# Every written order of a two-part kernel replaced by another: emission, engine sequences and the slots of rotating tiles

## The chip, the core and the metric

The kernel runs on one core of a Trainium2 chip. The metric is the time of one execution on the device in microseconds (us); the lower the better. Five engines take part: TensorE (PE, with its weight loads as PEld), VectorE (DVE), ScalarE (ACT), GpSimd (POOL) and SyncE (SP), which here only issues transfers. Each engine takes its instructions strictly in its own written order and waits, where data or a buffer is not there, with everything behind the waiting instruction.

## What is computed

Two independent results are put side by side. Part A is attention over a short window with 32 heads: each position looks at eight earlier positions, two apart. Part B is a convolution along the sequence whose kernel is a sum of 192 decaying complex exponentials per channel.

```python
def _A_ref(x, wqkv, wo):                    # x: 1 x 2048 x 640, 32 heads of 20
    q, k, v = ...                           # x @ wqkv
    idx = pos[:, None] - (jnp.arange(8) * 2)[None, :]
    logits = jnp.einsum("bhsd,bhswd->bhsw", q, kg) * scale
    attn = _softmax(jnp.where(mask, logits, -1e9), axis=-1)
    o = jnp.einsum("bhsw,bhswd->bhsd", attn, vg)
    return o @ wo

def _B_ref(u, A_re, A_im, B_re, B_im, C_re, C_im, log_dt, Dskip):
    logdA, dB = dt * A, dt * Bc             # 640 channels x 192
    P = jnp.exp(logdA[:, :, None] * l)      # l = 0 .. 2047
    K = jnp.einsum("dn,dnl,dn->dl", Cc, P, dB).real
    y = irfft(rfft(u padded) * rfft(K padded))[:L]
    return y + u * Dskip

return jnp.concatenate([a, b], axis=-1)
```

## The kernel before, in words

The program is cut into small pieces of work, each for one engine, and each belongs to a stage. A stage's name carries its block or chunk number: `logits2` is the attention logits of the third block of 512 positions, `kgen43` the fourth quarter of the convolution kernel of the fifth chunk of 128 channels.

Stages of part A: `x0..3` load the input transposed; `k`, `q`, `v` with a number project 512 positions (five groups of five matmuls and evictions each, line 747) and store them to device memory; `fetch` reads the q and k rows of a block back in five tiles through three rotating buffers (`qk`, line 767), `fetchv` the v rows (line 780); `logits` makes ten products on VectorE (line 793), which TensorE sums (line 800), then a maximum, an exponential and a division (lines 808 to 828); `av` makes ten products of v and the attention weights on VectorE (line 842), summed by TensorE (line 850); `out` is the output projection (line 867). The products of `logits` and `av` go through three rotating buffers (`pr`).

Stages of part B: `prep`, `weights`, `am0/am1`, `gens0/gens1`, `genm0/genm1` make the exponentials at powers of two: a phase and its absolute value on VectorE (lines 477 and 479), two sines on ScalarE (lines 478 and 480) and a product with the magnitude on VectorE (line 488). Set 0 is for the first chunk and stays on the chip, set 1 for the other four goes through device memory (`Gdram`). The temporary tiles of these stages rotate through four buffers (`tmp4`). For each chunk c of five, `tab` and `taby` read the generators back, `xtab` and `ypos` multiply them up to two tables (Xtab has two buffers, Ytab only one), `mag` and `yneg` add Ytab's other half (lines 557, 562 and 563). `kgen` (lines 596 and 603) contracts the tables on TensorE in four quarters of two pieces each; a piece is 64 small matmuls, the first with four more. `kd` shifts the result between partitions by four transfers (line 584); `spread` (lines 637, 642 and 658) and `spec` (lines 678 and 683) take it to the frequency domain, as `u` does with the input; `swap` exchanges halves by a transfer (line 1073); `prod` (lines 688 and 689) multiplies the spectra, `inv` (line 703) and the `last` stages (lines 1131 and 1134) go back, with constants that `hb` loads (HB, eight transfers of 512 KB, line 1103) and an input product `ud` (line 1112).

What sets the order is written out by hand in three constants. `TRACE` is the order in which pieces are emitted; it sets the program's data dependencies and which buffer a rotating tile follows. `SEQ` is each engine's order (`.P` TensorE, `.A` ScalarE, `.V` VectorE, `.G` GpSimd, `.S` SyncE; `:4` means four pieces in a row). `SLOTS` says, for each use of a rotating tile in the order of emission, which buffer it takes.

```python
    def slot(self, pool, tag, bufs, shape, dt, name):
        k = self.used.get(tag, 0)
        self.used[tag] = k + 1
        i = int(SLOTS[tag][k]) if tag in SLOTS else k % bufs
        return pool.tile(shape, dt, name=name, tag=f"{tag}{i}", bufs=1)
    ...
    def chain(self, text):
        ...
                for ins in next(left[stage, engine]):
                    if engine in last:
                        self.tc.add_manual_dep(ins, last[engine].name, ...)
                    last[engine] = ins
    ...
    op.trace(TRACE, dict(attpool=attention_pool, fftpool=fft_pool, invpool=inv_pool))
    op.chain(SEQ)
```

Three words in `TRACE` (`attpool`, `fftpool`, `invpool`) are places where a memory pool gives way to another.

Of the kernel before, what the change touches and what calls it, by code (L numbers as in the profile page):

```python
# [127 lines left out]
def att_consts_np():  # L128
# [13 lines left out]
ypos0.G params.A params.S params2.G params.A params.S params2.G params.A params.S params2.G params.A params.S params2.G params.A params.S  # L142
params2.G:2 params.S prep.A params.A params2.G prep.V x0.S params2.G:2 params.S params2.G prep.V:2 x0.S prep.V params2.G prep.V prep.P prep.V
params2.G prep.P prep.A x0.S params2.G weights.P mag0.A params2.G mag0.A:2 params2.G mag0.A x0.S prep.P mag0.A params2.G mag0.A prep.P mag0.A prep.V
mag0.A ypos0.G weights.P mag0.A wk.S load.G mag0.A prep.V load.G mag0.A x0.S weights.P prep.V mag0.A load.G mag0.A weights.P mag0.A prep.V mag0.A
load.G weights.P mag0.A x1.S weights.A prep.V load.G weights.P weights.A gens0.V load.G prep.V weights.P weights.A gens0.V x1.S load.G prep.V
weights.V weights.A weights.P am0.A load.G prep.V am0.A weights.V am0.A wq.S load.G am0.A:2 x1.S set.G weights.V am0.A set.G am0.A:2 weights.V
am0.A:2 load.G x1.S weights.V am0.A prep.A weights.V load.G k0.P weights.S gens1.V load.G x2.S gens1.V load.G gens0.A gens1.A load.G gens1.V gens0.A
k0.P load.G gens1.A gens1.V load.G x3.S gens1.A weights.V gens1.A gens1.V k0.P genm0.V k0.A gens1.V x1.S gens1.A q0.P weights.V k0.A wv.S gens1.A
gens1.V q0.P weights.V x2.S q0.A gens1.V q0.P gens1.A x2.S weights.V k0.A q0.P weights.V gens1.A gens0.V x2.S weights.V q0.A q0.P gens0.V gens0.A  # L150
gens0.V gens0.A gens0.V q0.A weights.S k0.P gens0.V genm0.V gens0.A x2.S gens0.V gens0.A gens0.V gens0.A k0.P genm0.V gens0.A gens0.V gens0.A
gens0.V gens0.A x3.S genm0.V k0.A gens0.V:2 k0.A genm0.V gens0.V gens0.A xtab0.V k0.S v0.P gens0.A v0.P gens0.A gens0.V x3.S xtab0.V gens0.A xtab0.V
q0.A gens0.V:2 v0.P q0.A genm0.V gens0.V gens0.A xtab0.V q0.S gens0.A:2 gens0.V k1.P x3.S xtab0.V gens0.A gens0.V gens0.A gens0.V gens0.A xtab0.V
gens0.V gens0.A k1.P genm0.V gens0.A x3.S genm0.V xtab0.V k1.P xtab0.V genm0.V v0.A xtab0.V k1.P v0.A xtab0.V genm0.V v0.A xtab0.V k1.P v0.P genm0.V
xtab0.V am1.A xtab0.V v0.P v0.A genm1.V am1.A xtab0.V genm1.S v0.A k1.A v0.S q1.P:2 k1.A genm1.V k1.A q1.P k1.A gens1.V k1.A xtab0.V q1.P am1.A k1.S
xtab0.V genm1.S am1.A xtab0.V q1.P am1.A genm1.V v1.P am1.A xtab0.V genm1.S q1.A v1.P q1.A gens1.V q1.A v1.P xtab0.V q1.A genm1.V q1.A v1.P am1.A
q1.S xtab0.V genm1.S am1.A gens1.V k2.P xtab0.V am1.A k2.P xtab0.V am1.A v1.A gens1.V k2.P am1.A xtab0.V v1.A k2.P xtab0.V v1.A ypos0.V v1.A k2.P
ypos0.V k2.A ypos0.V:2 k2.A v1.P k2.A:2 ypos0.V k2.A ypos0.V v1.A k2.S q2.P yneg0.V q2.P v1.S q2.P gens1.A ypos0.V gens1.A q2.P gens1.A gens1.V q2.P
genm1.V q2.A:2 gens1.V v2.P genm1.S q2.A:2 ypos0.V q2.A v2.P gens1.A q2.S v2.P gens1.A gens1.V genm1.V gens1.A v2.P gens1.V v2.A genm1.S v2.A v2.P
genm1.V gens1.A k3.P gens1.V v2.A genm1.S ypos0.V v2.A:2 k3.P gens1.V gens1.A v2.S q3.P gens1.V gens1.A genm1.V gens1.A q3.P gens1.V genm1.S gens1.A  # L160
q3.P genm1.V gens1.A k3.A gens1.V genm1.S q3.P q3.A genm1.V q3.A q3.P gens1.V q3.A genm1.S q3.A ypos0.V k3.P q3.A gens1.A q3.S yneg0.V v3.P gens1.A
v3.P k3.A genm1.V k3.A v3.P yneg0.V genm1.S attpool fetch0.S v3.P gens1.A mag1.A fetch0.S v3.A:2 v3.P v3.A mag1.A:2 kgen03.P tab1.S mag1.A:2 wo.S
mag1.A:2 fetch0.S mag1.A k3.P mag1.A logits0.V fetchv0.S mag1.A:2 fetchv0.S mag1.A k3.P mag1.A fetchv0.S logits0.V mag1.A:3 k3.A kgen03.P logits0.V
fetch0.S k3.A v3.A k3.S logits0.P v3.A kgen02.P xtab1.V kgen03.A v3.S fftpool logits0.V fetchv0.S xtab1.V:2 logits0.V xtab1.V:5 logits0.P xtab1.V
kgen00.P xtab1.V:2 kgen00.P logits0.V xtab1.V:2 logits0.V u0.S fetch0.S xtab1.V u0.S logits0.P kgen00.A kgen01.P xtab1.V:2 u0.S xtab1.V kgen01.P
xtab1.V logits0.V u0.S xtab1.V:2 logits0.V logits0.P fetch1.S kgen01.A kgen02.P xtab1.V:2 kgen02.A ypos1.G taby1.S logits0.V ypos1.G taby1.S:2
xtab1.V logits0.P taby1.S xtab1.V taby1.S logits1.V T.S u0.P logits0.A u0.P kd0.S u0.A u0.P ypos1.V kd0.S u0.P u0.A logits1.V fetch1.S u0.P u0.A
u0.P fetchv0.S u0.P u0.A kd0.S ypos1.V u0.P ypos1.V u0.A logits0.V kd0.S u0.A u1.S ypos1.V u0.A:2 logits0.V ypos1.V logits0.P ypos1.V logits0.V
ypos1.V logits0.P spec.P logits0.A spec.P:2 spec.A fetchv0.S spec.A ypos1.V spec.P spec.A:2 spec.P spec.A tab2.S spec.A spec.P spec.A wo.S spec.A
logits1.V spread0.P fetch1.S spread0.P spec.A spread0.P spread0.A spread0.P fetch1.S spread0.A ypos1.V u1.S spread0.A ypos1.V spec.A:3 logits0.P  # L170
yneg1.V spread0.A spec.P:2 spec.A spread0.P spec.A spread0.P:2 spread0.A spread0.P yneg1.V spread0.P spec.A spread0.P spec.A spread0.P logits0.A
spread0.P mag2.A logits0.P mag2.A xtab2.V mag2.A u1.S logits0.A yneg1.V logits0.A mag2.A xtab2.V mag2.A kgen13.P xtab2.V mag2.A logits0.V mag2.A:3
wo.S mag2.A kgen13.P xtab2.V mag2.A swap0.S mag2.A:2 xtab2.V fetchv0.S xtab2.V mag2.A xtab2.V mag2.A u1.S spread0.A xtab2.V spread0.A xtab2.V
# [132 lines left out]
010101001011  # L306
# [883 lines left out]
```

## Time and profile before

| | |
|---|---|
| median of three runs | 370.8 us (368.31, 371.45, 370.8) |
| span of the profiled execution, first to last instruction | 368.0 us |
| that execution's own time outside the span | not given; the lowest of the three runs is 0.3 us above the span |
| TensorE busy, mean granted clock | 292.8 us, 0.903 |
| VectorE busy | 305.1 us |
| ScalarE busy | 257.2 us |
| transfers | 65.5 MB, mean 178 GB/s |

In the rows shown below, a line of the timeline has the start and the duration in us, the engine, the source line, the operation with its output and inputs, how many instructions are merged, and in brackets the idle time of the engine ahead of it with what ended that wait. "issue" there is a wait for nothing that the profile shows. SPq is the queue of transfers that SyncE issues; L12 is line 12 of the kernel.

### The profile page before, as it was taken

What the parts mean: (1) busy time and instruction counts of PE and PEld (TensorE: products, weight loads), DVE (VectorE), ACT (ScalarE), POOL (GpSimd) and SP (SyncE); (2) the same over time, 40 slices, a digit from 0 to 9 for tenths busy, and PEclk for the clock granted to TensorE, in tenths of its full rate; (3) what the DMA queues carried; (4) which work ended last, traced back from release to release, by engine and by line L of the source; (5) the groups of instructions that cost most, each with busy time, mean ns of one, the idle gap of its engine ahead of it and who ended that gap; (6) DMA issues with size and microseconds to landing.
All of it is one profiled execution on the core that took longest, in us unless ns stands there. A gap on an engine that the chain in (4) does not pass through costs nothing. (4 is left out here: it accounts for less than half of the span.)

```text
span 368.0 us, 13345 instructions
## 1 busy us (share of the span) xinstructions
PE 292.8 (80%) x5808; PEld 195.3 (53%) x5808; DVE 305.1 (83%) x397; ACT 257.2 (70%) x574; POOL 35.6 (10%) x72
## 2 busy tenths in 40 slices
PE   2959999999654486777989796888988748889984
PEld 1414444445431375555666564567855546557763
DVE  1896999795899988998999998799999935568940
ACT  2978899898600588357999645797779304779773
POOL 9740000000000000000000000000000000002750
PEclk9978999999665678899999899997999966999999
DMA  7999683697978987566976355860768756999885
GB/s 152 204 205 213 185 269 117 202 287 228 263 140 147 238 210 134 139 161 95 205 99 156 121 133 109 228 150 15 142 213 235 257 209 101 190 219 192 227 191 136
DMA packets 119210, 65.49 MB, mean 178 GB/s; under 512 B 76192, under 2 KB 115712, under 8 KB 118000
## 3 DMA queue, kind: packets, MB, share of 16 engines
q1 hardware_dynamic: 116320, 61.61, 71.6%
q0 software_dynamic: 1776, 2.79, 3.7%
q8 instruction: 45, 0.74, 0.9%
q10 hardware_dynamic: 1056, 0.25, 0.3%
q14 instruction: 13, 0.11, 0.1%
HBM read 35.25 MB, written 21.03 MB: 153 GB/s over the span
## 5 line engine op out<-in xcount | busy, mean ns | idle before, releaser
L747 PE MATMUL ps_p<-xT,w 128*128 128x512 bf16 x300 | 69.9, 397 | 4.1 <-DMA w<-in_A_wqkv_dram 4.1
L603 PE MATMUL ps_k<-Ytab,Xtab 64*20 64x33 bf16 (+1 forms) x2560 | 52.9, 247 | 11.7 <-issue 11.7
L842 DVE TENSOR_TENSOR p<-vb,attn 128x2048 bf16<-128x2048 bf16 x40 | 47.5, 1218 | 12.4 <-PE ps_o L850 10.3
L603 PEld LDWEIGHTS <-Xtab 64*20 64x20 bf16 (+1 forms) x2560 | 47.6, 123 | 17.0 <-issue 14.7
L793 DVE TENSOR_TENSOR prod<-qk 128x2048 bf16<-128x2048 bf16 x40 | 48.1, 1224 | 10.0 <-DMA qk<-qkd 7.5
L747 PEld LDWEIGHTS <-w 128*128 128x128 bf16 x300 | 30.2, 102 | 43.0 <-issue 6.2
L683 ACT CAST Sp<-ps_f 128x512 bf16<-128x512 f32 (+1 forms) x96 | 43.1, 613 | 7.0 <-PE ps_f L678 6.7
L662 ACT CAST A<-ps_f 128x512 bf16<-128x512 f32 x80 | 41.4, 619 | 7.1 <-PE ps_f L658 6.8
L617 ACT CAST Kd<-ps_k 128x264 bf16<-128x264 f32 x20 | 7.9, 394 | 47.0 <-PE ps_k L603 47.0
L750 ACT CAST st<-ps_p 128x512 bf16<-128x512 f32 x60 | 31.7, 609 | 7.1 <-DMA qkd<-st 3.1
L800 PE MATMUL ps_l<-prod,cGs 128*32 128x512 bf16 x160 | 21.5, 464 | 17.2 <-DVE prod L793 17.1
L678 PE MATMUL ps_f<-A,cT 64*128 64x128 bf16 (+1 forms) x768 | 27.7, 214 | 7.3 <-ACT Sp L683 3.5
L678 PEld LDWEIGHTS <-cT 64*128 64x128 bf16 x768 | 21.6, 98 | 16.4 <-issue 11.3
L706 ACT CAST Z<-ps_ia 128x512 bf16<-128x512 f32 x40 | 21.7, 632 | 5.6 <-PE ps_ia L703 5.6
L850 PE MATMUL ps_o<-p,cHs 64*32 64x256 bf16 x640 | 21.7, 288 | 4.1 <-DVE p L842 4.1
L867 PE MATMUL ps_op<-wo,oT 128*128 128x320 bf16 x160 | 24.4, 300 | 0.3 <-ACT oT L856 0.2
L547 POOL MEMSET Ytab<- 128x192 bf16 x5 | 1.3, 258 | 238.3 <-PE ps_k L603 134.4
L557 ACT ACTIVATE mag<-ta 128x192 bf16<-128x192 f32 x80 | 22.8, 404 | 0.0
L1139 POOL DMA_DIRECT2D out_dram<-ys x24 | 14.4, 608 | 76.8 <-ACT rc L826 70.2
L703 PE MATMUL ps_ia<-cE,Sp 128*128 128x128 bf16 x160 | 20.5, 224 | 0.7 <-DVE Sp L689 0.4
L510 DVE TENSOR_TENSOR krtmp<-Xtab,Xg 128x3072 bf16<-128x3072 bf16 (+1 forms) x15 | 20.3, 1356 | 0.1
L703 PE MATMUL ps_ia<-cE,UT 128*128 128x128 bf16 x160 | 20.4, 224 | 0.0
(113 smaller groups left out, 531.3 us busy)
## 6 DMA issues: line engine op xcount, KB each, us to landing
qk<-qkd SPq DMA_DIRECT2D x20, 263.0 KB
qkd<-st SPq DMA_DIRECT2D x8, 640.0 KB
UT<-Sp SPq DMA_DIRECT2D x10, 512.0 KB
Gdram<-cs SPq DMA_DIRECT2D x11, 384.0 KB
HB<-k_HB SPq DMA_DIRECT2D x8, 512.0 KB
vb<-vd SPq DMA_DIRECT2D x16, 196.5 KB
Xg<-Gdram SPq DMA_DIRECT2D x4, 768.0 KB
Zdram<-Z SPq DMA_DIRECT2D x3, 1024.0 KB
```

The costliest lines, as they stand in the source:

```text
L557: self.op("A", lambda b=b: self.nc.scalar.activation(out=self.mg[b // 8]()[:, b % 8], in_=ta()[:, s], func=ACT.Exp, scale=-16.0 * (b + 1)))
L603: MM(ps()[32 * g:32 * g + 20, i, :], lhsT=X()[k, :, p % 2, col], rhs=Y()[k, :, p % 2, col], start=False, stop=(p == order[3]), tile_positi ...
L662: op("A", lambda q=q, ps=ps: nc.scalar.copy(out=A1()[:].rearrange("p k r s t -> p (k r) s t")[:, :, sig, 8 * q:8 * q + 8], in_=ps()[:]))
L678: nc.tensor.matmul(ps[h]()[:, kk], lhsT=C["T"]()[hs, k, 64 * (1 - r):64 * (1 - r) + 128], rhs=A1()[hs, k, r, s0:s1, :].rearrange("p s t -> ...
L683: op("A", lambda q=q, h=h, ps=ps: nc.scalar.copy(out=Sp()[:, slots, h, :, 4 * q:4 * q + 4], in_=ps[h]()[:].rearrange("p k (s t) -> p s t k ...
L703: nc.tensor.matmul(ps()[:, i], lhsT=X()[:, h, 4 * t:4 * t + 4, :].rearrange("p g k -> p (g k)"), rhs=C["E"]()[:, n_, :], start=(i == 0 and ...
L706: op("A", lambda h=h, tq=tq, ps=ps: nc.scalar.copy(out=Z()[:, :, 16 * h + 4 * tq:16 * h + 4 * tq + 4], in_=ps()[:].rearrange("p t x -> p x ...
L747: nc.tensor.matmul(ps()[:], lhsT=self.w[which]()[:, kt, 128 * ct:128 * ct + 128], rhs=self.xT()[:, kt, 512 * sc:512 * sc + 512], start=(kt ...
L750: op("A", lambda ct=ct, ps=ps: nc.scalar.copy(out=st()[:, ct], in_=ps()[:]))
L793: op("V", lambda ct=ct, wg=wg, pr=pr: V.tensor_tensor(out=pr[wg]()[:], in0=self.qk[b][ct]()[:, 0, HALO:].unsqueeze(1).to_broadcast([128, 4 ...
L842: op("V", lambda t=t, qp=qp, v4=v4: V.tensor_tensor(out=v4(), in0=windows(self.v[b][t]()[:, 2 * qp:2 * qp + 2, 0:PH], 2, 4), in1=at()[:].u ...
L867: nc.tensor.matmul(ps()[:], lhsT=self.oT[b]()[:, t, 128 * s:128 * s + 128], rhs=self.wo_sb()[:, t, 320 * eh:320 * eh + 320], start=(t == 0 ...
```

## The change

All of `TRACE` and `SEQ` is replaced, and the slot strings of `pr`, `ps`, `st` and `tmp4`. The pieces and their number are the same (432 for TensorE, 576 for ScalarE, 397 for VectorE, 68 for GpSimd, 269 for SyncE). `TRACE` is one line longer, so that later source lines are one higher. The diff is long; here are the parts of `SEQ` and `SLOTS` that the prediction speaks of.

```diff
 # TensorE, chunks 2 to 4
-...spread1.P:3 u2.P:6 out0.P u2.P:2 inv0.P:8 spec1.P out0.P:2 ... spec1.P:4 out0.P:2 kgen21.P:2
+spec1.P:2 logits1.P out0.P spec1.P logits2.P spec1.P:4 logits2.P spec1.P kgen22.P:2 kgen23.P:2 kgen20.P:2 kgen21.P:2 u3.P:6 inv1.P u3.P logits2.P u3.P
-...u4.P:5 kgen32.P:2 kgen30.P logits2.P kgen33.P:2 kgen30.P
-logits2.P:2 inv2.P logits2.P inv2.P:7 kgen31.P:2 u4.P:3 av1.P:2 ...
+...spec2.P:5 kgen30.P kgen31.P:2 u4.P kgen30.P kgen33.P:2
+u4.P:5 av1.P:2 inv2.P:4 u4.P av1.P kgen32.P:2 av1.P logits2.P:4 spread3.P:4 ...
-...spec3.P:8 av2.P:3 kgen43.P
-av2.P kgen42.P av2.P kgen40.P:2 kgen42.P kgen41.P:2 kgen43.P av2.P:3 inv3.P av2.P inv3.P logits3.P inv3.P:5 spread4.P:2 ...
+spec3.P av2.P kgen43.P kgen40.P:2 kgen41.P:2 kgen43.P kgen42.P av2.P:2 kgen42.P spec3.P av2.P spec3.P:2 av2.P spec3.P av2.P:3 inv3.P:3 av2.P inv3.P
+out2.P:2 logits3.P out2.P spread4.P:4 out2.P logits3.P out2.P spread4.P:6 logits3.P spread4.P:2 out2.P:3 inv3.P:4 spec4.P logits3.P spec4.P:3
 # ScalarE, start
-params.A:5 prep.A params.A prep.A mag0.A:16 weights.A:4 am0.A:11 prep.A gens0.A ...
+params.A:6 prep.A:2 am0.A:11 mag0.A:5 weights.A mag0.A:11 gens0.A:3 prep.A gens0.A:2 ...
 # VectorE: start, first logits, end
-prep.V:11 gens0.V prep.V gens0.V prep.V weights.V prep.V weights.V:5 ...
+prep.V:10 gens0.V:4 prep.V gens0.V prep.V gens0.V prep.V gens0.V prep.V ...
-... gens1.V ypos0.V yneg0.V genm1.V yneg0.V logits0.V:3
+... genm1.V:2 ypos0.V yneg0.V ypos0.V:2 yneg0.V logits0.V:3 yneg0.V logits0.V
-... yneg4.V:3 av2.V:5 prod3.V:4 av2.V logits3.V:10 ud1.V ud0.V logits3.V:3 prod4.V:4 ud2.V logits3.V ud3.V av3.V:10
+... av2.V yneg4.V av2.V yneg4.V av2.V:2 logits3.V av2.V:5 prod3.V:3 av2.V prod3.V logits3.V:5 ud1.V ud0.V logits3.V:4 ud2.V ud3.V logits3.V:3 prod4.V:4 logits3.V av3.V:10
 # SyncE, HB and the shift of chunk 4
-fetchv3.S:4 hb.S:8 ud.S:2 kd4.S:2 ud.S kd4.S:2 fetch3.S ud.S:2 fetch3.S ...
+fetchv3.S:3 hb.S:4 ud.S kd4.S:2 hb.S:2 ud.S:2 kd4.S:2 hb.S:2 ud.S:3 fetch3.S out2.S ...
 # SLOTS
     "pr":
-01201020102010212012012102102010201021012020120201201201201201201020102012012012
+01201020102010201201201020120120102010201102102102102102121212102010201021021021
     "tmp4":
-012301010120312012031203120312031203120312031203120312
+012301230231023102320323120213012301230123012301230123
```

A "half" of `kgen` in the prediction is one piece: half of a quarter's work.

More of the change, by code (lines that the diff above doesn't have):

```diff
@@ L141 @@
 TRACE = """
[L142 to L149, printed above, removed]
@@ L154 @@
[L154 to L161, printed above, removed]
@@ L268 @@
-xtab4.V:2 logits2.V xtab4.V logits2.V xtab4.V:2 prod2.V xtab4.V:2 prod2.V av1.V logits2.V xtab4.V:2 av1.V xtab4.V prod2.V xtab4.V:2 prod2.V xtab4.V
-logits2.V xtab4.V:4 av2.V xtab4.V:2 av2.V:2 xtab4.V:4 ypos4.V:8 av2.V ypos4.V:2 yneg4.V:3 av2.V:5 prod3.V:4 av2.V logits3.V:10 ud1.V ud0.V
-logits3.V:3 prod4.V:4 ud2.V logits3.V ud3.V av3.V:10 ypos0.G params2.G:16 ypos0.G load.G:9 set.G:2 load.G:7 ypos1.G:2 ypos2.G:2 ypos3.G:2 ypos4.G:2
-last01.G:4 last03.G:3 last11.G:4 last03.G last05.G:4 last13.G:4 last07.G:4 params.S:6 x0.S params.S x0.S:3 wk.S x0.S x1.S:2 wq.S x1.S:2 weights.S
```

260 lines of the change are left out of this document (139 added, 121 removed).

## The prediction, made before the changed kernel ran

> **What bounds the kernel now.** I read the page first, then VectorE's instructions in order of time with the idle time ahead of each, then the same for TensorE, ScalarE and the SyncE queue around every hole, and last the chain that ended last.
>
> ```profile
> span 368.0 us, 13345 instructions
> ...
> PE 292.8 (80%) x5808; PEld 195.3 (53%) x5808; DVE 305.1 (83%) x397; ACT 257.2 (70%) x574; POOL 35.6 (10%) x72
> ...
> DVE 19%; PE 14%; DMA 7%; issue 5%; SPq 3%; ACT 1%; ACTq 0%; DVEq 0%
> ```
>
> VectorE is the fullest engine and leads the chain. As no operation changes, its 305.1 us of work stay, and only its 62.9 us of idle time (368.0 - 305.1) can move. So the prediction is a ledger of VectorE's holes plus what follows its last instruction.
>
> ```profile
> 5.79 0.28 DVE L427 CAST dtf<-dtb 128x5 f32<-128x5 bf16 x1 [5.79 <-ACT dtb L426]
> ...
> 351.88 2.36 DVE L842 TENSOR_TENSOR p<-vb,attn 128x2048 bf16<-128x2048 bf16 x2 [0.33 <-PE ps_o L850]
> 364.38 0.33 ACTq L1185
> ```
>
> VectorE starts at 5.8 and ends at 354.2 (351.88 + 2.36). The last 13.8 us are TensorE's remaining products, ScalarE's last evictions and the stores. Between them lie some 43 us of holes; the parts below take the large ones. The same ledger would be wrong where TensorE or ScalarE is the later one, so each hole is judged by the engine it waits for.
>
> **The change part by part.** Every sequence differs, so I compare the places where VectorE waits. "Cover" is the VectorE work that the written order puts between the instruction that starts a round trip through other engines and the one that needs its result; the hole is round trip minus cover.
>
> *Opening, to the first attention product.*
>
> ```profile
> 13.25 0.60 DVE L435 TENSOR_SCALAR wk<-ps_tr 128x448 f32<-128x448 f32 x1
> ...
> 29.17 0.26 DVE L477 TENSOR_SCALAR ph<-wi 128x192 int32<-128x192 int32 x1 [0.75 <-ACT cs L478]
> ...
> 36.52 0.26 DVE L477 TENSOR_SCALAR ph<-wi 128x192 int32<-128x192 int32 x1 [1.37 <-ACT Xg L478]
> ...
> 86.34 0.96 DVE L488 TENSOR_TENSOR cs<-cs,am 128x1536 bf16<-128x1536 bf16 x1 [0.52 <-ACT cs L480]
> ...
> 92.30 3.57 DVE L793 TENSOR_TENSOR prod<-qk 128x2048 bf16<-128x2048 bf16 x3 [4.13 <-DMA qk<-qkd]
> 96.69 0.56 DVE L510 TENSOR_TENSOR krtmp<-Xg 128x768 bf16<-128x768 bf16 x1 [0.81 <-DMA Xg<-Gdram]
> ```
>
> ```profile
> 88.50 0.95 SPq L767 DMA_DIRECT2D qk<-qkd  x2
> ```
>
> The last genm1 product ends at 87.3; SyncE stores it, then issues the qk fetch at 88.5, and the first product starts at 92.3. The round trip is 5.0 us, and the old order covers it with one instruction (yneg0's third), so 4.13 stay open, and 0.81 more for Xg, fetched behind it. The new order puts five instructions there (the last three of ypos0 and two of yneg0, some 6.3 us), and the fetch still stands right behind genm1's last store. I book -4.9.
>
> Against it: the new order takes gens0 first, and its second range reduction (wk) takes a tmp4 buffer that the first gens0 phase must give back, which needs a sine on ScalarE.
>
> ```profile
> 8.80 4.15 ACT L557 ACTIVATE mag<-ta 128x192 bf16<-128x192 f32 x16
> ...
> 14.65 2.90 ACT L465 ACTIVATE am<-ta 128x192 bf16<-128x192 f32 x11
> ...
> 17.98 1.28 ACT L478 ACT_TABLE_LOAD   x1
> ```
>
> In the new order am0, mag0 and one cast (0.6) stand ahead of the sines: 8.8 + 2.9 + 4.15 + 0.6 + 1.3 = 17.7, so the first sine ends near 18.1. VectorE gets there at 14.5 (13.25 plus two phases and two absolute values), because the weights products that filled this time before now come later. That is a new hole of 3.6, and 1.0 more while ScalarE paces the sines; the old holes at 29.17 and 36.52 (2.1) go. Net +2.5. The opening: -4.9 + 2.5 = -2.4 (bounds -4.9 with all of it covered, +1.5 if ScalarE's pace costs 5 instead of 1).
>
> *Middle, to the end of yneg4.*
>
> ```profile
> 129.61 1.23 DVE L793 TENSOR_TENSOR prod<-qk 128x2048 bf16<-128x2048 bf16 x1 [0.93 <-DMA qk<-qkd]
> ...
> 138.99 1.23 DVE L828 TENSOR_TENSOR attn<-attn,rc 128x1024 bf16<-128x1024 bf16 x1 [1.61 <-ACT rc L827]
> ...
> 171.58 0.56 DVE L510 TENSOR_TENSOR krtmp<-Ytab 128x768 bf16<-128x768 bf16 x1 [1.68 <-DMA Ytab<-Gdram]
> ...
> 225.48 0.56 DVE L510 TENSOR_TENSOR krtmp<-Ytab 128x768 bf16<-128x768 bf16 x1 [0.89 <-DMA Ytab<-Gdram]
> ...
> 231.97 1.23 DVE L842 TENSOR_TENSOR p<-vb,attn 128x2048 bf16<-128x2048 bf16 x1 [2.06 <-PE ps_l L800]
> ```
>
> These are 7.2 us. The loop behind two of them is yneg(c) -> kgen(c) on TensorE -> taby(c+1) into the single Ytab -> ypos(c+1). The prices:
>
> ```profile
> 247.68 2.48 PE L603 MATMUL ps_k<-Ytab,Xtab 128*20 128x33 bf16 x128
> ```
>
> ```profile
> 270.40 0.43 SPq L543
> ...
> 270.88 3.90 DMA Ytab<-Gdram
> ```
>
> A kgen half is 1.3 us where TensorE runs free (2.48 for the products of two, with its opening matmuls); the reload is 0.4 + 3.9. For chunk 2 the new order runs all eight halves together: 8 x 1.3 + 4.3 = 14.7 against 21.6 of cover, so the wait at ypos3 goes; at ypos2 the last half stands ahead of 11.5 of cover, so that wait goes too. For chunk 3 the loop holds six halves (I take 10, between 7.8 free and 12.0 at the slowest pace shown below), six u4, three av1 and four inv2 products (some 6.1) and two more halves (2.6): with the reload 23.0 against 21.9 of cover, a hole of 1.1, which I raise to 2.0 for the start. For chunk 0 it is about even (0.5). The softmax wait of 1.61 stays (cover 11.2, before 10.7), the waits at 129.61 and 231.97 go, and I allow 0.8 for a new one of their kind: 2.0 + 0.5 + 1.6 + 0.8 = 4.9, so -2.3 (bounds -5.6 and +4).
>
> *kgen4.* The dearest hole.
>
> ```profile
> 286.19 0.97 DVE L563 TENSOR_SCALAR Ytab<-Ytab 128x3072 bf16<-128x3072 bf16 x1
> 287.08 5.76 DVE L842 TENSOR_TENSOR p<-vb,attn 128x2048 bf16<-128x2048 bf16 x5
> ...
> 296.41 1.23 DVE L689 TENSOR_TENSOR Sp<-Sp 128x2048 bf16<-128x2048 bf16 x1
> 307.57 1.23 DVE L842 TENSOR_TENSOR p<-vb,attn 128x2048 bf16<-128x2048 bf16 x1 [9.93 <-PE ps_o L850]
> ```
>
> ```profile
> 286.19 5.31 SPq L1103 DMA_DIRECT2D HB<-k_HB  x8
> ```
>
> ```profile
> 199.98 2.32 PE L603 MATMUL ps_k<-Ytab,Xtab 64*20 64x33 bf16 x119
> ...
> 207.40 0.44 PE L603 MATMUL ps_k<-Ytab,Xtab 64*20 64x33 bf16 x13 [1.95 <-issue]
> ...
> 296.19 2.14 PE L603 MATMUL ps_k<-Ytab,Xtab 64*20 64x33 bf16 x116 [3.71 <-issue]
> ...
> 301.84 2.51 PE L603 MATMUL ps_k<-Ytab,Xtab 64*20 64x33 bf16 x128 [3.19 <-issue]
> ```
>
> VectorE had nine instructions to do (five av2, four prod3) and then waited 9.93 for a product buffer, held until TensorE had worked through kgen4. TensorE itself stood 3.71 and 3.19 with no wait that the profile shows, while 4 MB of HB came in. Without HB four halves in a row still took 7.9 us (199.98 to 207.84), 2.0 each: back to back, kgen does not hold 1.3. The new order has seven halves in a row and only three VectorE instructions (3.45 at the pitch of 287.08) to lay over them; four of the eight HB loads come, some 4 us later than before. I take 11.5 for the seven (9.1 free, 14.0 at 2.0). One av2 product and the start add 0.9, so 11.5 + 0.9 - 3.45 = 8.9; behind it spec3's last four now stand between the av2 products that free the buffers, 2.6 more. 11.5 against 9.93: +1.6 (bounds -1 and +6).
>
> *End.*
>
> ```profile
> 316.95 3.68 DVE L793 TENSOR_TENSOR prod<-qk 128x2048 bf16<-128x2048 bf16 x3 [2.47 <-PE ps_l L800]
> 322.73 2.36 DVE L793 TENSOR_TENSOR prod<-qk 128x2048 bf16<-128x2048 bf16 x2 [2.10 <-DMA qk<-qkd]
> ...
> 332.57 0.42 DVE L813 SCALAR_TENSOR_TENSOR m<-m,ps_m 128x256 bf16<-128x256 bf16 x1 [3.75 <-PE ps_m L812]
> ...
> 338.21 1.48 DVE L1112 TENSOR_TENSOR uD<-uD,Dsb 128x2560 bf16<-128x2560 bf16 x1
> ```
>
> Two uD products (2.8 at pitch) leave the stretch between prod4 and av3 for these holes: -2.8. But prod4 waits for spec4, and between the last spread4 product and spec4's first the new TensorE order puts three out2 and four inv3 groups (some 4.3) where one logits3 and one out2 group stood (1.4); the old order has four more out2 groups among spec4's own, so of these 2.9 I book +1.8. Together -1.0 (bounds -4 and +4), and +0.5 for the end behind av3, where TensorE, not VectorE, is the later one.
>
> **The sum:** -2.4 - 2.3 + 1.6 - 1.0 + 0.5 = -3.6, so 364.4 against the span of 368.0. The three runs shown have a median of 370.8, 2.8 above that span (the lowest, 368.3, is 0.3 above); what is around the span does not change, so 370.8 - 3.6 = 367.2.
>
> [...]
>
> ```profile
> q8 instruction: 45, 0.74, 0.9%
> ```
>
> 45 code pages of 16 KB came in. [...]
>
> **The rivals.**
> 1. *kgen at 1.3 everywhere*, the stalls being accidents of that one execution. Then the seven halves take 9.1 (-2.4) and the holes at ypos4 and ypos1 close (-2.5): 367.2 - 4.9 = 362.3. For it: the free pair at 247.68. Against: the stall at 207.40 had no HB beside it.
> 2. *Slower: chunk 4 is starved.* HB's loads delay TensorE's code and chunk 4's shifted rows. The eight halves of before took 19.2 us without the av2 products between them (286.2 to 306.6), 2.4 each; seven at 2.4 are 16.8, +5.3. The second half of the Kd shift now stands on SyncE behind six HB and three uD loads; two HB and two uD (1.66 MB, 9.3 us at the page's mean of 178 GB/s) come right ahead of it, and TensorE has only some 11.4 us of other work before spread4, against 14: +2.6. The six halves of kgen3 at 2.0 add 2.0, kgen0 0.2. 367.2 + 10.1 = 377.3. It decides from some 4 us of issue stalls inside kgen4. For it: both stalls of 3 us and more lie under HB. Against: HB now starts later and in parts.
> 3. *The holes form anew*: the written order is obeyed, but the waits it closes in the middle and the opening come back elsewhere, as each engine takes its order as written however late a transfer is. Without -2.4 and -2.3: 371.9.
>
> **How the numbers follow.** My forecast 0.42 (its own range 363 to 371), rival 1 0.16, rival 2 0.30, rival 3 0.12. A measurement of this kernel can tell about 1% (3.7 us) from no change. The forecast lies on that bound: 0.22 faster, 0.18 within, 0.02 slower. Rival 1 is faster, rival 2 slower, rival 3 0.02, 0.07 and 0.03. Together 0.40 faster, 0.25 same, 0.35 slower. The range runs from 357 (rival 1 with opening and end at their lower bounds: 362.3 - 2.5 - 3.0) to 379 (rival 2 and a third of the end's upper bound).
>
> **What would show it.** Opening: the first product (now line 794) starts near 90 with no wait for qk, and a hole of about 3.6 at 14 to 18. Middle: no wait for Ytab at ypos2 and ypos3, one of about 2 at ypos4. kgen4: seven halves in 11 to 12 us and a hole of 9 behind three VectorE instructions. If these seven take over 15, rival 2 holds; if 9, rival 1. The forecast is wrong in kind if VectorE's holes sum to what they were but lie in places not named here, or if TensorE's end stands far behind VectorE's.

## The result, and the profile after

The changed kernel is slower: 380.01 us median of four runs (379.26 to 382.78) against 370.58 us for before (with a fourth run, 370.36, beside the three listed above), a ratio of 1.0291 with a 95% interval of 1.0226 to 1.0355. Measured again on another chip it stood at 1.0215 (1.0165 to 1.0265). The forecast was 367.2 us, with a range up to 379.0: wrong in sign, and outside the range by 1 us. The ratios here leave out executions that took over 1.5% longer than the fastest of the same kernel (8 of the 12 of early_again, further down), so some differ from the quotient of the medians.

The page of after, span, busy time, chain and two groups of instructions:

```profile
span 377.5 us, 13318 instructions
...
PE 297.8 (79%) x5808; PEld 198.9 (53%) x5808; DVE 304.4 (81%) x397; ACT 258.6 (69%) x574; POOL 35.9 (10%) x72
...
PE 36%; ACT 21%; DMA 16%; DVE 15%; issue 8%; SPq 2%; POOL 1%; ACTq 0%; DVEq 0%; POOLq 0%
...
L604 PE MATMUL ps_k<-Ytab,Xtab 64*20 64x33 bf16 (+1 forms) x2560 | 53.7, 247 | 20.2 <-issue 20.2
L843 DVE TENSOR_TENSOR p<-vb,attn 128x2048 bf16<-128x2048 bf16 x40 | 47.6, 1220 | 23.1 <-PE ps_o L851 18.1
```

The same two groups on the page of before:

```profile
L603 PE MATMUL ps_k<-Ytab,Xtab 64*20 64x33 bf16 (+1 forms) x2560 | 52.9, 247 | 11.7 <-issue 11.7
L842 DVE TENSOR_TENSOR p<-vb,attn 128x2048 bf16<-128x2048 bf16 x40 | 47.5, 1218 | 12.4 <-PE ps_o L850 10.3
```

VectorE's work is the same (304.4 us, in before 305.1). Its idle time over the span grew by some 10 us (from 62.9 to 377.5 - 304.4 = 73.1), and the av products alone account for as much (12.4 to 23.1), most of it behind one TensorE result, ps_o. The chain is now led by TensorE, which stood 8.5 us longer for "issue" in kgen.

VectorE in after, in order of time:

```profile
85.48 3.49 DVE L794 TENSOR_TENSOR prod<-qk 128x2048 bf16<-128x2048 bf16 x3
...
93.29 1.23 DVE L794 TENSOR_TENSOR prod<-qk 128x2048 bf16<-128x2048 bf16 x1 [3.46 <-PE ps_l L801]
...
158.61 1.23 DVE L794 TENSOR_TENSOR prod<-qk 128x2048 bf16<-128x2048 bf16 x1 [4.25 <-PE ps_l L801]
...
286.14 0.95 DVE L564 TENSOR_SCALAR Ytab<-Ytab 128x3072 bf16<-128x3072 bf16 x1
287.01 2.35 DVE L843 TENSOR_TENSOR p<-vb,attn 128x2048 bf16<-128x2048 bf16 x2
289.40 1.23 DVE L794 TENSOR_TENSOR prod<-qk 128x2048 bf16<-128x2048 bf16 x1
307.74 2.36 DVE L843 TENSOR_TENSOR p<-vb,attn 128x2048 bf16<-128x2048 bf16 x2 [17.10 <-PE ps_o L851]
```

The first attention product starts at 85.48, 6.8 us earlier than in before (92.30). Half of that lead goes at once, in 3.46 us of waiting for a sum of TensorE. By the end of yneg4 all of it is gone: 286.14 + 0.95 = 287.1, against 287.2. Then comes the hole of kgen4: 17.10 us, where before had 9.93. VectorE leaves it at 307.6 in before and 307.7 in after, but before had done five av2 and four prod3 instructions ahead of it, after only three instructions.

TensorE at chunk 3's spread and in kgen4, in after:

```profile
267.59 0.87 PE L823 MATMUL ps_n<-attn,cSm 128*128 128x256 bf16 x4 [0.47 <-ACT attn L818]
273.31 1.90 PE L638 MATMUL ps_s<-Kd,cSEL 128*32 128x256 bf16 x36 [4.86 <-DMA Kd<-Kd]
...
292.40 2.30 PE L604 MATMUL ps_k<-Ytab,Xtab 128*20 128x33 bf16 x114 [0.99 <-issue]
...
297.22 2.52 PE L604 MATMUL ps_k<-Ytab,Xtab 64*20 64x33 bf16 x128 [2.15 <-issue]
302.60 1.11 PE L604 MATMUL ps_k<-Ytab,Xtab 128*20 128x33 bf16 x52 [2.85 <-issue]
```

and at that spread in before:

```profile
267.80 2.35 PE L867 MATMUL ps_op<-wo,oT 128*128 128x320 bf16 x16 [0.23 <-ACT oT L856]
271.19 1.06 PE L637 MATMUL ps_s<-Kd,cSEL 128*32 128x256 bf16 x36 [1.05 <-DMA Kd<-Kd]
```

SyncE's queue around it, after first, then before:

```profile
265.41 2.87 SPq L544 DMA_DIRECT2D Ytab<-Gdram  x5
268.38 3.43 SPq L585 DMA_DIRECT2D Kd<-Kd  x4
```

```profile
265.89 3.91 SPq L584 DMA_DIRECT2D Kd<-Kd  x4
269.92 2.34 SPq L543 DMA_DIRECT2D Ytab<-Gdram  x5
```

Both kernels end kgen3 near 265.4. Before shifts Kd at once and has four out1 groups for TensorE meanwhile (267.80). After reloads Ytab first, shifts Kd 2.5 us later, and TensorE stands 4.86 us with nothing written in between. So TensorE comes to the end of yneg4 late: in after the first spec3 group starts at 284.5, in before at 278.3 and the last is done at 285.1. The windows view tells what is left from yneg4's end to the end of the program. A row has the length, the busy time of PE, PEld, DVE, ACT and POOL with the number of their instructions, then the granted clock, the mean busy share of the DMA engines and GB/s. Before, then after:

```profile
287.16:368.04 80.88, 61.91 (x1464) 46.96 (x1463) 47.78 (x43) 45.44 (x106) 14.42 (x24) 0.92 0.85 195
```

```profile
287.09:377.49 90.40, 71.01 (x1646) 52.99 (x1644) 50.28 (x44) 53.52 (x122) 14.41 (x24) 0.89 0.87 204
```

TensorE of after has 182 matmuls more to do, among them five spec3 groups of 16 and four av2 groups of 16, and is busy 9.1 us longer with what is left. VectorE is not quite level either: it has two av2 products more (2.5 us). A ledger of VectorE's holes does not show that debt.

Two stretches ahead of it by the same view, before and then after:

```profile
240.00:270.00 30.00, 27.08 (x791) 21.81 (x785) 30.00 (x40) 24.80 (x61) 0.45 (x2) 0.89 0.50 122
270.00:287.00 17.00, 13.90 (x302) 10.32 (x300) 16.50 (x19) 15.25 (x34) 0.00 (x0) 1.00 0.67 181
```

```profile
240.00:270.00 30.00, 25.48 (x770) 20.32 (x769) 27.32 (x39) 20.40 (x46) 0.45 (x2) 0.78 0.31 83
270.00:287.00 17.00, 13.61 (x202) 10.78 (x203) 17.00 (x18) 12.13 (x27) 0.00 (x0) 0.82 0.78 188
```

From 270 to 287 TensorE is busy about as long in both, but does 202 matmuls instead of 302. The mix differs (after has inv2 groups there, before more spec3 groups and the first products of kgen4), and the granted clock is 0.82 instead of 1.00; how much each of the two does was not parted.

### The profile page after: what moved, and what is told of

It is laid out like the page before. It is cut to its first block, busy times and chain, and to the rows that moved or that the text cites. A ratio compares the mean times of both kernels' runs of the same rounds, so it can differ in the third digit from the quotient of the medians.

```text
span 377.5 us, 13318 instructions
## 1 busy us (share of the span) xinstructions
PE 297.8 (79%) x5808; PEld 198.9 (53%) x5808; DVE 304.4 (81%) x397; ACT 258.6 (69%) x574; POOL 35.9 (10%) x72
## 4 chain that ended last, share of the span: by engine, by line
PE 36%; ACT 21%; DMA 16%; DVE 15%; issue 8%; SPq 2%; POOL 1%; ACTq 0%; DVEq 0%; POOLq 0%
PE ps_k L604 8%; PE ps_p L748 7%; PE ps_f L659 4%; ACT A L663 4%; DMA qkd<-st 4%; PE ps_f L679 3%; DMA out_dram<-ob 3%; PE ps_o L851 3%; ACT Sp L684 3%; DVE prod L794 3%; ACT st L751 3%; PE ps_op L868 3%; DVE Xtab L521 3%; DMA zb<-Zdram 3%; ACT mag L558 2%
## 5 line engine op out<-in xcount | busy, mean ns | idle before, releaser
L604 PE MATMUL ps_k<-Ytab,Xtab 64*20 64x33 bf16 (+1 forms) x2560 | 53.7, 247 | 20.2 <-issue 20.2
L843 DVE TENSOR_TENSOR p<-vb,attn 128x2048 bf16<-128x2048 bf16 x40 | 47.6, 1220 | 23.1 <-PE ps_o L851 18.1
L794 DVE TENSOR_TENSOR prod<-qk 128x2048 bf16<-128x2048 bf16 x40 | 48.3, 1222 | 11.5 <-PE ps_l L801 9.7
L663 ACT CAST A<-ps_f 128x512 bf16<-128x512 f32 x80 | 42.6, 634 | 13.0 <-PE ps_f L659 12.8
L679 PE MATMUL ps_f<-A,cT 64*128 64x128 bf16 (+1 forms) x768 | 31.2, 230 | 7.7 <-ACT Sp L684 5.8
L679 PEld LDWEIGHTS <-cT 64*128 64x128 bf16 x768 | 24.2, 106 | 17.0 <-issue 16.1
L851 PE MATMUL ps_o<-p,cHs 64*32 64x256 bf16 x640 | 24.2, 295 | 3.1 <-DVE p L843 1.6
L707 ACT CAST Z<-ps_ia 128x512 bf16<-128x512 f32 x40 | 21.9, 646 | 4.9 <-PE ps_ia L704 4.8
L704 PE MATMUL ps_ia<-cE,Sp 128*128 128x128 bf16 x160 | 21.7, 231 | 4.0 <-DVE Sp L690 1.9
L704 PE MATMUL ps_ia<-cE,UT 128*128 128x128 bf16 x160 | 21.6, 230 | 0.0
L659 PE MATMUL ps_f<-cBU,U 128*64 128x256 bf16 x160 | 17.8, 363 | 4.7 <-issue 2.3
```

The source lines that it names most:

```text
L604: MM(ps()[32 * g:32 * g + 20, i, :], lhsT=X()[k, :, p % 2, col], rhs=Y()[k, :, p % 2, col], start=False, stop=(p == order[3]), tile_positi ...
L659: nc.tensor.matmul(ps()[n * h:n * h + n, :, 4 * j:4 * j + 4], lhsT=sv()[:, :, 2 * q + j], rhs=C[mat]()[:].rearrange("p (k g) -> p k g", g= ...
L663: op("A", lambda q=q, ps=ps: nc.scalar.copy(out=A1()[:].rearrange("p k r s t -> p (k r) s t")[:, :, sig, 8 * q:8 * q + 8], in_=ps()[:]))
L679: nc.tensor.matmul(ps[h]()[:, kk], lhsT=C["T"]()[hs, k, 64 * (1 - r):64 * (1 - r) + 128], rhs=A1()[hs, k, r, s0:s1, :].rearrange("p s t -> ...
L704: nc.tensor.matmul(ps()[:, i], lhsT=X()[:, h, 4 * t:4 * t + 4, :].rearrange("p g k -> p (g k)"), rhs=C["E"]()[:, n_, :], start=(i == 0 and ...
L794: op("V", lambda ct=ct, wg=wg, pr=pr: V.tensor_tensor(out=pr[wg]()[:], in0=self.qk[b][ct]()[:, 0, HALO:].unsqueeze(1).to_broadcast([128, 4 ...
```

## The experiments

Each kernel below computes the same outputs by the same operations; only the written order differs. In all of them the rotating PSUM banks and buffers were dealt out again by one rule, the one released first, so the slot strings differ a little from after's as well (after_again is after itself, unchanged).

### Grafts: which part of the order costs

Orders joined at one piece: all that stands up to it in one kernel's emission, then the rest in the other's.

```diff
 head_new:     after up to logits0's first product, then before
 head_old:     before up to logits0's first product, then after
 to_yneg4_new: after up to yneg4's last instruction, then before
 to_yneg4_old: before up to yneg4's last instruction, then after
```

> The order of after up to its first attention product (logits0), and from there the rest in the order of before; banks and buffers dealt out again in order of release. Theory 1 (the loss is TensorE's: it falls behind where kgen halves stand in rows of four to eight, in chunks 0 to 3, and pays in the tail): the opening of after is sound, VectorE keeps most of its 6.8 us, 363 to 366 us. Theory 2 (the loss is made in the tail alone, by the order around kgen4): the same, 363 to 366. Theory 3 (the opening's gain is no gain: TensorE has done some 8 us less work by 92 us and must do it later): 369 to 372.

> The mirror image: the order of before up to its first attention product, then the rest in the order of after. Theory 1: the middle and the tail of after cost some 13 us together and the opening's gain is missing too, 383 to 388 us. Theory 2: the same, as both lie behind the cut. Theory 3 (the opening's gain was no gain): 378 to 381, as after.

> The order of after up to the last instruction of yneg4, and the tail in the order of before. VectorE ended yneg4 at 287.1 in after and 287.2 in before. Theory 1: the four spec3 products, two av2 products and four out1 groups that TensorE has not done by then are owed whatever the tail's order, so most of the loss stays, 376 to 380 us. Theory 2: the tail's order is the cause, and with the old one the time is that of before, 369 to 372.

> The order of before up to the last instruction of yneg4, and the tail in the order of after. Theory 1: TensorE comes to the tail with nothing owed, so the tail's order costs little, 370 to 374 us. Theory 2: the tail's order costs its 9.5 us, 378 to 381.

| kernel | ratio to before (95%) |
|---|---|
| head_new | 1.0133 (0.9997 to 1.0268) |
| head_old | 1.0336 (1.0251 to 1.0421) |
| to_yneg4_new | 1.0261 (1.0172 to 1.0349) |
| to_yneg4_old | 1.0139 (1.0047 to 1.0232) |

With before's tail behind after's first 287 us the loss stays (1.0261): the tail's order is not its main cause, as theory 1 said. Behind before's head the new tail still costs 1.4%, between what theory 1 (370 to 374 us, up to 1.009 times 370.6) and theory 2 (378 to 381, from 1.020) had named. No gain from the opening could be measured: with the old one in its place the time is 1.0336 against 1.0291, intervals overlapping, although its qk wait is back (3.60 us in the trace). head_old does not decide between the theories: 1.0336 is just where theory 1 began (383 of 370.6 us is 1.0335), and its interval also reaches theory 3's 378 to 381 us (1.020 to 1.028). head_new tells less than it should, since the joint made a wait of its own:

```profile
99.41 0.57 DVE L511 TENSOR_TENSOR krtmp<-Xg 128x768 bf16<-128x768 bf16 x1 [10.00 <-DMA Xg<-Gdram]
```

### One piece, or one row of loads, moved

```diff
 kgen32_early, TensorE (ScalarE's eviction of kgen32 likewise)
-kgen33.P:2 u4.P:5 av1.P:2 inv2.P:4 u4.P av1.P kgen32.P:2 av1.P
+kgen33.P:2 u4.P:3 kgen32.P:2 u4.P:2 av1.P:2 inv2.P:4 u4.P av1.P:2
 kgen2_spread, TensorE (ScalarE's evictions of u3 likewise)
-kgen22.P:2 kgen23.P:2 kgen20.P:2 kgen21.P:2 u3.P:6 inv1.P u3.P logits2.P u3.P
+kgen22.P:2 u3.P:2 kgen23.P u3.P:2 kgen23.P u3.P kgen20.P u3.P kgen20.P u3.P:2 kgen21.P:2 inv1.P logits2.P
 hb_late, SyncE
-hb.S:4 ud.S kd4.S:2 hb.S:2 ud.S:2 kd4.S:2 hb.S:2 ud.S:3
+kd4.S:4 ud.S:3 hb.S:8 ud.S:3
 kgen2_row, on before, TensorE (ScalarE's evictions likewise)
-kgen22.P u3.P:2 logits2.P u3.P:4 kgen23.P logits2.P kgen22.P u3.P:2 kgen23.P
+kgen22.P kgen23.P kgen22.P kgen23.P u3.P:2 logits2.P u3.P:4 logits2.P u3.P:2
```

> after, with one thing moved: the last kgen piece of chunk 3 (both halves and the eviction) stands three u4 groups behind kgen33, instead of behind all of u4, three av1 and four inv2 groups. In after TensorE then waited 4.86 us at spread3 for the shifted Kd (1.05 in before). Theory 1 (what TensorE loses on the way to yneg4 is what is owed in the tail): the wait falls below 1.5 us and the ratio from 1.029 to about 1.018 to 1.024. Theory 2 (VectorE sets the time there, the wait of TensorE is free): the wait falls, the ratio stays at 1.026 to 1.032.

> after, with one thing moved: the eight u3 groups and their evictions stand between the eight halves of kgen2 instead of behind them (TensorE and ScalarE orders alone). In after the eight halves ran from 201.1 to 218.3 with 7.2 us of issue stalls inside, 4.68 of it in one half. Theory 1 (halves in a row ask for code pages faster than they come): the stalls inside kgen2 fall below 2.5 us, halves and u3 together end some 4 to 5 us earlier, and the ratio to before goes from 1.029 to about 1.017 to 1.022. Theory 2 (stalls are accidents or come from data traffic): 6 to 8 us of stalls stay and the ratio stays 1.026 to 1.032.

> after, with one thing moved: all eight HB loads and the first three uD loads stand behind the four Kd shifts of chunk 4 on SyncE, so that no HB comes in while kgen4 runs. In after the seven halves in a row took 15.7 us with 6.7 us of issue stalls. Theory 1 (the row itself outruns the code pages): the stalls stay, 5 to 8 us, and the seven halves take 14.5 to 17 us; the ratio stays within 0.4% of 1.029, a little lower since the second half of the shift comes some 5 us earlier. Rival 2 as predicted (HB holds up the code): the stalls fall below 3 us, the seven halves to 10 to 12, the ratio to about 1.016.

> before, with one thing moved: the eight halves of kgen2 stand in a row, as in after; the u3 groups and one logits2 group that parted three of them come behind. In before the first five, in a row, had 2.97 us of issue stalls, the three parted ones none. Theory 1 (the row makes the stalls): 5 to 8 us of stalls inside kgen2, and 0.5 to 1% slower than before. Theory 2 (accidents, data traffic): about 3 us as in before and the same time.

| kernel | ratio to before (95%) | issue stalls inside the moved kgen |
|---|---|---|
| kgen32_early | 1.0045 (1.0007 to 1.0083) | as in after |
| kgen2_spread | 1.0212 (1.0164 to 1.0260) | kgen2: 3.5 us, after 7.2 |
| hb_late | 1.0356 (1.0303 to 1.0410) | kgen4's seven halves: 4.7 us, after 6.7 |
| kgen2_row | 1.0112 (1.0072 to 1.0152) | kgen2: 5.3 us, before 3.0 |

The stalls are the steps of over 0.3 us from one matmul's start to the next inside the halves.

By its time kgen32_early takes away most of the loss, more than either theory had given it. Its rows, SyncE, then TensorE:

```profile
258.78 2.24 SPq L544 DMA_DIRECT2D Ytab<-Gdram  x5
261.12 4.43 SPq L585 DMA_DIRECT2D Kd<-Kd  x4
```

```profile
267.07 1.90 PE L638 MATMUL ps_s<-Kd,cSEL 128*32 128x256 bf16 x36 [0.50 <-DMA Kd<-Kd]
```

The 4.86 us became 0.50. Its VectorE still has a hole of 13.32 us in kgen4 (17.10 in after, 9.93 in before), so the size of that hole was no measure of the loss.

hb_late speaks against the reason that rival 2 gave. Without any HB load kgen4 still stalls, and its seven halves take 13.7 us (288.4 to 302.0) against 15.7:

```profile
291.26 2.30 PE L604 MATMUL ps_k<-Ytab,Xtab 128*20 128x33 bf16 x114 [0.92 <-issue]
...
295.53 2.52 PE L604 MATMUL ps_k<-Ytab,Xtab 64*20 64x33 bf16 x128 [1.59 <-issue]
299.54 1.11 PE L604 MATMUL ps_k<-Ytab,Xtab 128*20 128x33 bf16 x52 [1.49 <-issue]
```

The three shown stalls sum to 4.0 us against 5.99 in after's rows. By the table's count they are 4.7 against 6.7, between what theory 1 (5 to 8) and rival 2 (below 3) had named, so HB could have a share of up to 2 us. But the same seven halves with HB took 12.9 us in kd3_first (below), 14.0 in kgen2_spread and 14.9 in after_again, so that share lies inside the spread of executions. The ratio of hb_late can't be read for this question, because it made a new wait of its own:

```profile
331.63 2.90 DVE L1113 TENSOR_TENSOR uD<-uD,Dsb 128x2560 bf16<-128x2560 bf16 x2 [8.03 <-DMA uD<-in_B_u_dram]
```

kgen2_spread halved its stalls, and its time lies inside what after itself measured (1.0215 and 1.0291): no gain shown. kgen2_row got more stalls, as theory 1 said, and is slower; but it also holds up a logits2 product (4.36 us of VectorE's idle time there), so the 1.1% is not the price of the stalls alone.

### Combinations, and the tail by itself

```diff
 kd3_first, on after, SyncE
-taby4.S:5 kd3.S:4
+kd3.S:4 taby4.S:5
 kgen4_spread, on after, TensorE (evictions likewise; prod3.V:4 ahead of av2's fifth product)
-kgen43.P kgen40.P:2 kgen41.P:2 kgen43.P kgen42.P av2.P:2 kgen42.P spec3.P av2.P spec3.P:2 av2.P spec3.P
+kgen43.P kgen40.P spec3.P kgen40.P spec3.P kgen41.P spec3.P kgen41.P spec3.P kgen43.P av2.P kgen42.P av2.P kgen42.P av2.P:2
 two_moves = kgen32_early + kgen2_spread
```

> after itself, beside the three variants of it and before on one chip. All theories: 1.023 to 1.035 times before.

> after, with one thing moved: on SyncE the four shifts of chunk 3's Kd stand ahead of the five Ytab loads of chunk 4, as they do in before; the memsets that open that Ytab move with it. No engine's order changes. Theory 1 (TensorE's lateness counts: its 4.86 us at spread3 are owed in the tail): the wait at spread3 falls to about 1.5 to 2.5, the hole at ypos4 grows from 1.2 to about 4.5, and the time falls all the same, ratio 1.012 to 1.022 against 1.029. Theory 2 (VectorE's Ytab loop counts, and kgen32_early gained by its earlier Ytab): the same two movements, and the time stays or rises, ratio 1.029 to 1.040.

> after, with the tail changed alone: spec3's last four products and their evictions stand between the halves of kgen4 instead of behind them, two av2 products parted likewise, and the four prod3 products on VectorE ahead of av2's fifth. In after the halves stalled 6.7 us and VectorE waited 17.1 us with three instructions in hand. Theory 1 (stalls come of halves in a row, and what TensorE owes has to be done anyway): stalls inside kgen4 fall to 2 to 4 us, VectorE has prod3 to do in the hole, and the ratio falls from 1.029 to about 1.016 to 1.022. Theory 2 (the written order of the tail costs nothing beside the lateness): within 0.4% of 1.029.

> kgen2_spread and kgen32_early together, on after. If the two gains (0.8% and 2.5%) add up: ratio 0.992 to 1.000 to before. If the earlier end of kgen2 is lost in the wait for what chunk 3 has late: 1.002 to 1.007, as kgen32_early alone.

| kernel | ratio to before (95%) |
|---|---|
| after_again | 1.0215 (1.0165 to 1.0265) |
| kd3_first | 1.0272 (1.0212 to 1.0332) |
| kgen4_spread | 1.0253 (1.0201 to 1.0306) |
| two_moves | 1.0042 (1.0009 to 1.0075) |

On one chip, then, after is at 1.0215 and two_moves at 1.0042, and two_moves stands where kgen32_early alone stood: the parted kgen2 adds nothing that can be seen, although its stalls inside kgen2 fell to 1.0 us. kd3_first and kgen4_spread had their buffers dealt out by the same rule and gained nothing, so that is not what two_moves gained by. The tail's order by itself (kgen4_spread) brings no gain either, though the stalls inside its halves fell to 3.3 us (in a profiled execution of 386.6 us). kd3_first spoke against theory 1 as I had put it. TensorE and VectorE in it:

```profile
272.54 1.90 PE L638 MATMUL ps_s<-Kd,cSEL 128*32 128x256 bf16 x36 [2.20 <-DMA Kd<-Kd]
```

```profile
273.82 0.56 DVE L511 TENSOR_TENSOR krtmp<-Ytab 128x768 bf16<-128x768 bf16 x1 [4.53 <-DMA Ytab<-Gdram]
```

The wait for Kd fell to 2.20, the one for Ytab rose from 1.20 to 4.53, and nothing was won. The last half of kgen3 releases two chains, and SyncE's order only chooses which of them is late.

### Parting the two chains

```diff
 early_again, early_third = kgen32_early
 early_kd_first, early_kd_first2 = kgen32_early, with kd3.S:4 ahead of taby4.S:5
 early_kd_late = kgen32_early, with kgen32's eviction behind logits2's second exponential on ScalarE
 early_old_tail = kgen32_early up to yneg4's last instruction, then before
```

> kgen32_early itself, as the reference for the three beside it. All theories: 1.001 to 1.008 times before.

> kgen32_early with the four Kd shifts of chunk 3 ahead of the five Ytab loads on SyncE: the shift about 2 us earlier still, the reload some 4 us later, about where after had it. If Kd for TensorE carries the gain: at most 1.007 times before. If the Ytab reload for VectorE carries it: 1.014 to 1.025. If both must be early: 1.008 to 1.016.

> kgen32_early with the eviction of that piece four evictions later on ScalarE (behind logits2's two exponentials), so that the Ytab reload stays early and the Kd shift comes about when after had it: TensorE again waits 4 to 5 us at spread3. If Kd for TensorE carries the gain: 1.016 to 1.026 times before. If the Ytab reload carries it: at most 1.008. If both must be early: 1.008 to 1.016.

> kgen32_early up to the last instruction of yneg4, and the tail in the order of before. If the tail's order counts once TensorE comes to it on time (to_yneg4_old: 1.4% for the new tail behind the old head): 0.988 to 0.998 times before, faster than both kernels. If the tails are alike: 1.001 to 1.008, as kgen32_early.

> early_kd_first again, beside early_third. If Kd for TensorE carries the gain, as the profiles have it (spread3 starts 23.3 us behind kgen30's start in both, 26.3 in early_kd_late): within 0.4% of early_third, so about 1.002 to 1.010 times before. If both must be early: 1.015 to 1.026.

> kgen32_early a third time, as the reference beside it: 1.002 to 1.009 times before.

The times, with the stretch from the first product of kgen30 to the end of the last out3 product in the profiled execution. But for before and two_moves (whose kgen2 is another), these orders are alike up to kgen30 (early_old_tail's up to yneg4), and the stretch leaves out what an execution had gained or lost ahead of it (kgen30 starts between 243.5 and 249.6). Before starts kgen3 with kgen32, at 247.56.

| kernel | ratio to before (95%) | kgen30 to end, us |
|---|---|---|
| before | 1 | 115.5 |
| after, after_again | 1.0291, 1.0215 | 126.8, 126.7 |
| kd3_first | 1.0272 | 128.5 |
| early_kd_late | 1.0276 (1.0207 to 1.0345) | 127.1 |
| early_kd_first | 1.0261 (1.0183 to 1.0340) | 122.8 |
| early_kd_first2 | 1.0200 (1.0146 to 1.0255) | 123.7 |
| kgen32_early | 1.0045 | 122.6 |
| early_again | 1.0068 (1.0004 to 1.0132) | 122.4 |
| early_third | 1.0134 (1.0065 to 1.0202) | 121.8 |
| two_moves | 1.0042 | 122.0 |
| early_old_tail | 1.0231 (1.0184 to 1.0277) | 124.0 |

The rows that bound the stretch, in after and in kgen32_early (373.39 - 246.58 and 366.10 - 243.51):

```profile
246.58 0.30 PE L597 MATMUL ps_k<-Ytab,zw 128*32 128x264 bf16 x4
...
371.19 2.20 PE L868 MATMUL ps_op<-wo,oT 128*128 128x320 bf16 x15
```

```profile
243.51 0.30 PE L597 MATMUL ps_k<-Ytab,zw 128*32 128x264 bf16 x4
...
363.90 2.20 PE L868 MATMUL ps_op<-wo,oT 128*128 128x320 bf16 x15
```

The stretch by the windows view, in before, after and kgen32_early:

```profile
247.56:363.06 115.50, 97.02 (x2427) 74.45 (x2426) 86.88 (x93) 76.57 (x179) 14.88 (x26) 0.91 0.76 181
```

```profile
246.58:373.39 126.81, 103.85 (x2509) 79.33 (x2506) 89.55 (x92) 79.43 (x180) 14.87 (x26) 0.87 0.73 172
```

```profile
243.51:366.10 122.59, 103.22 (x2509) 78.35 (x2506) 89.88 (x92) 78.93 (x180) 14.87 (x26) 0.86 0.74 179
```

After takes 11.3 us longer than before here: TensorE is busy 6.8 us longer and idle 4.5 us longer (length minus busy time, 23.0 against 18.5). The moved piece gives back 4.2 us, nearly all of it idle time (19.4). The busy part stays. At the start of kgen3 TensorE of after and of all these variants has 80 matmuls more to do than before's, by their lines two u4 groups of 8 and four av1 groups of 16 (the rows above also count up to three that began earlier), and its granted clock is lower (0.87 against 0.91). So the moved piece is worth 4 to 5 us by the stretch (4.7 from after_again to two_moves), and the times on one chip give it 1.7%, some 6 us; that it is most of the loss holds for the times alone.

With Ytab early and Kd late, TensorE waits as in after and the gain is gone:

```profile
275.91 1.47 PE L638 MATMUL ps_s<-Kd,cSEL 128*32 128x256 bf16 x28 [4.81 <-DMA Kd<-Kd]
```

That Kd must be early is shown, by stretch (127.1) and by time (1.0276 beside early_again's 1.0068 on the same chip). With Kd early and Ytab about where after had it, the stretch keeps the gain (122.8 and 123.7), but the times (1.0261, 1.0200) do not separate it from after, and they lie where they were expected if the reload counts, not where Kd alone would have put them. The profile of early_kd_first is of the fastest of six executions (373.5 to 385.2 us), and in both profiles VectorE goes through ypos4 without a wait for Ytab, so these runs made no late Ytab to test. Whether Kd alone is enough stays open. early_old_tail was to beat both kernels and did not: before's tail puts all of spec3 ahead of kgen4, and TensorE, still owing four of its groups and waiting 3.56 us for a ScalarE eviction among them, starts kgen4 at 294.2, where early_again starts it at 284.6.

No version faster than before was found. kgen32_early comes nearest, at 1.0045, 1.0068 and 1.0134 on three chips.

## Why the prediction was wrong, step by step

- **Opening (-2.4).** The step was right and too small: no qk wait, the hole at the second range reduction 2.80 us (3.6 predicted), the first product 6.8 us earlier. What failed is to book it against the span. TensorE's work was not earlier (up to 92.3 us it had been busy 72.6 us in after, 80.4 in before), and a lead of VectorE alone ended in waits for TensorE (3.46 us at 93.29 and 4.25 at 158.61).
- **Middle (-2.3): the step that failed.** At yneg4's end VectorE stood at the same time in both kernels, with two av2 products more still to do, where -4.7 had been booked. I priced the two late kgen halves of chunk 3 by the Ytab reload alone: 23.0 against 21.9 of cover, a hole of 2.0, measured 1.20. The same halves also release the Kd shift, then spread3, spec3 and all that TensorE does before kgen4. The prediction had said that each hole must be judged by the later engine, and did not follow TensorE from there: it put the wait at spread3 (4.86 us, 1.05 in before) at nothing. With this piece moved the loss went from 2.15% to 0.42% on the chip that ran both (after_again and two_moves, whose other move showed no effect), and the stretch from kgen30 to the end became 4 to 5 us shorter. The 80 matmuls that TensorE owed already at the start of kgen3 had no term in the sum either.
- **kgen4 (+1.6).** Mis-sized: the seven halves took 15.7 us (11.5 booked, 14.0 as the bound; 12.9 was the least of any execution with this row) and the hole was 17.1 (8.9 booked). The price is not the hole, though: kgen32_early has a hole of 13.3, to_yneg4_old of 12.9. Part of this miss is the tail's own, since to_yneg4_old is at 1.0139.
- **End (-1.0, and +0.5 behind av3).** av3 ended 9.2 us later. VectorE came out of the hole at the same time as in before, but with four prod3 instructions and five av2 products more to do, and one logits3 product less: 41 instructions and 46.8 us of work against 33 and 37.4. Behind av3 came 14.0 us, 13.8 in before.
- **Rival 2** named the place where the loss shows, and its mark, seven halves in over 15 us, was reached (but 14.9 in after_again, as slow a kernel). Its 377.3 us is 2.7 below the time measured; that it came so near is luck, as its reasons were not borne out. Without HB the halves still stalled (4.7 us in hb_late), and spread4 did not wait for the Kd shift at all (its first product in after, at 324.03, has no idle time of TensorE ahead of it). It had 0.30 for a loss of which the larger part was there before kgen4.
- **Rivals 1 and 3.** No execution came near rival 1's 9.1 us for the seven halves. Rival 3 (the closed waits come back elsewhere) is what became of the -4.7 up to yneg4; its 371.9 us kept the forecast's terms for kgen4 and the end, which fell short.
- **The last step of the sum** put 2.8 us around the span. Every execution of after shows 1.8 (379.26 against 377.5), so the forecast should have been some 366.2; beside the rest this is small.

Still open is what makes up the remaining 0.5 to 1.3% of kgen32_early. Its TensorE also has four spec3 groups left at yneg4's end, and the 80 matmuls owed at the start of kgen3 are there as in after. That this earlier debt is what remains is argued, not shown: no run took it away, and the lower granted clock is not parted from it.

## What to carry to other kernels

When the order of several engines changes, follow every chain that a moved piece releases, not only the one that ends at the fullest engine, and compare at each milestone what every engine has still to do. Here a lead of 6.8 us on one engine was worth nothing, as the engine that it waited for did not have it too. And the longest hole can mark where a debt is paid, not where it was made: graft the two orders together at a few joints before explaining it.

## What the runs showed of the hardware

Small matmuls in a row stood still for issue here, and the stalls went with the row. In after, with eight kgen halves in a row, kgen2 stalled 7.2 us; with u3 groups between them it stalled 1.0 us in two_moves and 3.5 in kgen2_spread, which has the same order there. Two rows of after and one of two_moves:

```profile
210.39 0.82 PE L604 MATMUL ps_k<-Ytab,Xtab 128*20 128x33 bf16 x36 [4.45 <-issue]
...
213.85 0.85 PE L604 MATMUL ps_k<-Ytab,Xtab 64*20 64x33 bf16 x40 [0.74 <-issue]
```

```profile
217.63 1.67 PE L604 MATMUL ps_k<-Ytab,Xtab 64*20 64x33 bf16 x79 [0.42 <-issue]
```

These stalls are not accidents of one execution: of 14 executions whose kgen2 stands in this row, ten waited 4.45 us ahead of the same matmul, the other four 1.3 to 4.2. The second of after's stalls did not come with data traffic. The windows view of after has the DMA engines at a mean share of 0.02 in that stretch, and the granted clock at 0.50 behind the long wait:

```profile
211.00:218.30 7.30, 5.74 (x284) 5.04 (x272) 7.30 (x9) 0.76 (x2) 0.00 (x0) 0.50 0.02 6
```

In after 20.2 us of TensorE's time went to issue waits in kgen, 11.7 in before. That code is what is waited for, as one theory of kgen2_spread and of hb_late has it, was not shown. During the wait of 4.45 us the DMA engines were at a share of 0.85, so for that one traffic is not ruled out. What was shown is that these waits can lie off the path: two_moves has 13.7 us of them, kgen32_early 19.5, at the same ratio.
